# Summing k's features: four tiles added on GpSimd, and attention's period in three equal rounds

## The chip, the cores and the metric

The kernel runs on one core of one Trainium2 chip. A core has a matrix engine (TensorE, PE in the profile, with its weight loads listed apart as PEld), three engines for elementwise work (VectorE or DVE, ScalarE or ACT, GpSimd or POOL) and a queue on SyncE (SP) from which this kernel issues all of its DMA transfers. The engines run side by side, each through its own list of instructions in order, and wait for each other on semaphores. The metric is the device time of one launch in microseconds, lower is better. Before the change it is 1194.68 us, the median of three runs (1191.11 to 1195.12).

## What is computed

Linear attention with a feature map of exponentials over 8 batches of 8 heads, and on its output a two-layer block.

```python
def phi(x):
    proj = np.einsum('bhsd,df->bhsf', x, w_phi)
    proj = proj - np.max(np.abs(proj), axis=-1, keepdims=True)
    return np.concatenate([np.exp(proj), np.exp(-proj)], axis=-1)
q_p, k_p = (phi(q), phi(k))                      # q, k, v: (8, 8, 576, 64); 2 x 128 features
kv  = np.einsum('bhsf,bhsd->bhfd', k_p, v)
z   = np.sum(k_p, axis=2)                        # the feature sums
num = np.einsum('bhsf,bhfd->bhsd', q_p, kv)
den = np.einsum('bhsf,bhf->bhs', q_p, z)[..., None] + 1e-06
x   = num / den                                  # gathered to 4608 x 512
h   = x @ w_in                                   # 512 -> 2048
out = (h - np.tanh(h)) @ w_out                   # 2048 -> 512
```

The change concerns `z`, and the order in which attention's work is issued. The block behind it is computed as before.

## The kernel before

**Units and tiles.** Attention is cut into 32 units of two heads (`e` = 0, 1). q and k of a unit lie transposed in one tile `qk`, 64 rows for each head, with 1152 columns: 576 of q and then 576 of k, which is nine tiles of 128 positions. Tiles 0 to 3 are q; tile 4 is half q's last 64 positions and half k's first 64; tiles 5 to 8 are k.

**What a unit goes through.** `project` multiplies position tiles with `w_phi` into a PSUM tile `pp`, whose one buffer holds a round of up to four tiles of both heads. Behind the products VectorE takes the largest magnitude of each row (`m`, line 207) and subtracts it (`t`, line 209), and only then may the next round overwrite `pp`. There are three rounds, of four, two and three tiles. `q_side` turns q's four and a half tiles on TensorE (`ptr`, `ptt`) and takes their exponentials into `qe` on ScalarE; `k_exp` takes k's into `kp`, which has five tiles (0 is the half one, valid in rows 64 to 127) times two signs of 128 features. `kv` (line 246) multiplies v with `kp` into `pc`. `ksum` (line 254) makes the feature sums as products of a block of ones with each of the five tiles of `kp`, four products of 128 columns for each tile (two heads times two signs), 20 in all, into the third quarter of `pc`. ScalarE copies both out (`kvt`, `kst`), `turn` transposes them on TensorE, and VectorE copies the turned tile into `kv` (line 279). `num` (line 291) and `denom` (line 306) multiply `qe` with that. The denominators travel to another layout and back by DMA: `dd` to `dn`, one reciprocal on VectorE (`den_recip`, lines 334 and 335), `rn` to DRAM (`rr`), and from there spread over the partitions (`rb`). On POOL `den_mul` (line 344) multiplies the numerators `d` with `rb`, and `x_store` writes the result to DRAM.

**The weights.** `w_in` and `w_out` arrive as 64-bit floats. In each period one tile of 128x512 is decoded to float32: one step on ScalarE (`dec_0`), three on VectorE (`dec_1`, lines 166 to 168) and a fourth (`dec_2`, line 172). The first 14 decoded tiles are also split into a high and a low part during attention (`split_w`): ScalarE rounds, POOL subtracts (line 93).

**The order.** Attention runs under a manual schedule, so the lists of all engines are what `period(i)` writes down. Period i does rounds 0 to 2 of unit i, kv and q's side of unit i-1, numerators and denominators of unit i-2, and the division of unit i-3. The feature sums of unit i-1 are the last thing on TensorE in period i; their copy and turn fall into the next period, so `turn` handles the products of unit i-1 and the sums of unit i-2 together, and VectorE's copy of them comes ahead of round 2. On POOL a period has the division and, in the first 14, the subtraction of the weight split. On SP a period has `dn`'s load, the next unit's `qk`, the store of x, `rr`, the two `rb` loads, `v`, and the next raw weight tile.

**Buffers that matter.** `ps_d` has three PSUM banks for everything short-lived (`ptr`, `ptk`, `pd`, `po`). `t2` (the subtracted k tiles of round 2) has one buffer; `d` and `rb` have two.

**Behind attention** the two-layer block runs 192 steps (12 groups of three token tiles, 16 slices of the hidden width), in which the remaining weight tiles are split.

## Time and profile before

One execution was profiled. It took 1192.87 us; its trace spans 1191.1 us from the first to the last instruction, at a mean granted TensorE clock of 0.999.

| stretch | length, us | PE busy | DVE busy | ACT busy | POOL busy |
|---|---|---|---|---|---|
| attention, 100 to 150 us | 50 | 48.90 | 40.81 | 35.85 | 10.78 |
| attention, 250 to 300 us | 50 | 49.32 | 39.92 | 32.07 | 7.07 |
| change of stage, 380 to 400 us | 20 | 16.45 | 17.55 | 12.46 | 14.72 |
| second stage, 600 us to the end | 591 | 585.79 | 419.71 | 404.98 | 143.27 |

The first product of the second stage starts at 371.52 us. The line numbers are those of the kernel before. In the views below a row gives a start and a duration in microseconds, the engine, the line, the operation with output and inputs, and in square brackets how long the engine stood idle ahead of it and who ended that. "x40" behind a product of four-byte floats counts two passes for each of 20 products. PEld rows are weight loads, which run beside products. A product is quoted with the rows and columns of the array that it uses: 64\*128 is half the rows.

### The profile page before, as it was taken

What the parts mean: (1) busy time and instruction counts of PE and PEld (TensorE: products, weight loads), DVE (VectorE), ACT (ScalarE), POOL (GpSimd) and SP (SyncE); (2) the same over time, 40 slices, a digit from 0 to 9 for tenths busy, and PEclk for the clock granted to TensorE, in tenths of its full rate; (3) what the DMA queues carried; (4) which work ended last, traced back from release to release, by engine and by line L of the source; (5) the groups of instructions that cost most, each with busy time, mean ns of one, the idle gap of its engine ahead of it and who ended that gap; (6) DMA issues with size and microseconds to landing.
All of it is one profiled execution on the core that took longest, in us unless ns stands there. A gap on an engine that the chain in (4) does not pass through costs nothing.

```text
span 1191.1 us, 22549 instructions
## 1 busy us (share of the span) xinstructions
PE 1164.2 (98%) x8584; PEld 974.0 (82%) x8584; DVE 883.9 (74%) x1458; ACT 807.4 (68%) x1748; POOL 288.4 (24%) x266
## 2 busy tenths in 40 slices
PE   7999999999998999999999999999999999999998
PEld 5666666666766879999999999999999999999997
DVE  6888887778785988777776777777776777777665
ACT  4667766666766767677766667677766667677665
POOL 0122221011112663222222222222222222222222
PEclk9999999999999999999999999999999999999999
DMA  4465566656552101000100101010100101000000
GB/s 160 146 200 185 178 198 184 182 188 201 170 176 87 33 13 41 14 34 14 35 20 8 40 14 40 14 35 14 36 19 7 40 15 40 14 28 1 28 2 26
DMA packets 51180, 85.70 MB, mean 72 GB/s; under 512 B 13312, under 2 KB 28032, under 8 KB 51072
## 3 DMA queue, kind: packets, MB, share of 16 engines
q1 hardware_dynamic: 51072, 84.27, 22.6%
q8 instruction: 67, 1.10, 0.4%
q14 instruction: 41, 0.34, 0.1%
HBM read 65.08 MB, written 19.02 MB: 71 GB/s over the span
## 4 chain that ended last, share of the span: by engine, by line
PE 87%; DVE 7%; issue 2%; ACT 1%; POOL 1%; DMA 1%; SPq 0%; DVEq 0%; POOLq 0%; ACTq 0%
PE ph L479 32%; PE po L516 11%; PE po L514 11%; PE po L513 11%; PE pp L202 7%; PE pc L246 5%; PE po L291 4%; PE pc L254 3%; PE pd L306 3%; DVE t L209 2%; DVE m L207 2%; PE ptt L215 1%; DVE s L496 1%; DVE dec_ai L167 0%; DVE s L500 0%
## 5 line engine op out<-in xcount | busy, mean ns | idle before, releaser
L507 POOL TENSOR_TENSOR gl<-s,gh 128x384 fp32r<-128x384 f32 x192 | 197.0, 1026 | 568.1 <-ACT gh L506 563.8
L479 PE MATMUL ph<-xh,wli 128*128 128x384 f32 x768 | 259.6, 338 | 1.3 <-POOL wli L93 1.3
L479 PE MATMUL ph<-xh,whi 128*128 128x384 f32 x768 | 259.1, 337 | 0.0
L479 PE MATMUL ph<-xl,whi 128*128 128x384 f32 x768 | 258.1, 336 | 0.0
L486 ACT ACTIVATE y<-ph 128x384 f32<-128x384 f32 x192 | 94.4, 492 | 238.2 <-PE ph L479 238.2
L495 DVE SCALAR_TENSOR_TENSOR s<-s,y 128x384 f32<-128x384 f32 x192 | 107.2, 559 | 166.8 <-ACT s L488 166.7
L513 PE MATMUL po<-who,gh 128*128 128x512 f32 x576 | 227.6, 395 | 1.6 <-ACT gh L506 1.6
L514 PE MATMUL po<-wlo,gh 128*128 128x512 f32 x576 | 227.3, 395 | 0.0
L516 PE MATMUL po<-who,gl 128*128 128x512 f32 x576 | 164.3, 393 | 4.4 <-POOL gl L507 4.4
L500 DVE COPY_PREDICATED s<-mk,th 128x384 f32<-128x384 uint32 x192 | 140.8, 733 | 20.1 <-DVE th L499 0.5
L479 PEld LDWEIGHTS ph<-xh,whi 128*128 128x128 f32 x768 | 144.6, 188 | 8.9 <-issue 0.5
L479 PEld LDWEIGHTS ph<-xl,whi 128*128 128x128 f32 x768 | 144.3, 188 | 8.3
L479 PEld LDWEIGHTS ph<-xh,wli 128*128 128x128 f32 x768 | 144.2, 188 | 2.0 <-POOL wli L93 1.9
L207 DVE TENSOR_REDUCE m<-pp 128x8 f32<-128x1024 f32 (+2 forms) x96 | 91.6, 954 | 65.1 <-PE pp L202 65.1
L516 PEld LDWEIGHTS po<-who,gl 128*128 128x128 f32 x576 | 107.9, 188 | 30.5 <-POOL gl L507 5.7
L496 DVE SCALAR_TENSOR_TENSOR s<-s,s 128x384 f32<-128x384 f32 x192 | 116.0, 604 | 21.2 <-ACT s L490 1.8
L513 PEld LDWEIGHTS po<-who,gh 128*128 128x128 f32 x576 | 108.3, 188 | 20.3 <-ACT gh L506 3.2
L514 PEld LDWEIGHTS po<-wlo,gh 128*128 128x128 f32 x576 | 108.5, 188 | 16.4
L490 ACT ACTIVATE s<-y,bias_t 128x384 f32<-128x384 f32 x192 | 117.9, 614 | 4.7 <-POOL gl L507 4.5
L494 ACT ACTIVATE mk<-y,bias_t 128x384 f32<-128x384 f32 x192 | 117.7, 613 | 2.8 <-DVE s L500 2.8
L488 ACT ACTIVATE s<-y,bias_t 128x384 f32<-128x384 f32 x192 | 118.4, 617 | 0.0
L344 POOL TENSOR_TENSOR rb<-d,rb 128x576 f32<-128x576 f32 x32 | 45.9, 1433 | 292.0 <-DMA rb<-rr 253.7
(66 smaller groups left out, 1640.1 us busy)
## 6 DMA issues: line engine op xcount, KB each, us to landing
qk<-in_qkT SPq DMA_DIRECT2D x31, 576.0 KB, 5.8
v<-in_v SPq DMA_DIRECT2D x32, 320.0 KB, 3.6
rb<-rr SPq DMA_DIRECT2D x64, 144.0 KB, 3.4
xs<-rb SPq DMA_DIRECT2D x32, 288.0 KB, 2.1
x<-xs SPq DMA_DIRECT2D x48, 192.0 KB, 2.3
out<-o SPq DMA_DIRECT2D x36, 256.0 KB, 2.0
rawi<-in_moe_w_in SPq DMA_DIRECT2D x16, 512.0 KB, 4.6
rawo<-in_moe_w_out SPq DMA_DIRECT2D x16, 512.0 KB, 4.4
```

Source lines behind the costliest of these rows:

```text
L207: nc.vector.tensor_reduce(m, x, AX.X, ALU.max, apply_absolute_value=True)
L479: nc.tensor.matmul(h, wt[:, c * P : (c + 1) * P], x[:, c, 0:N], start=(i == 0), stop=(i == 3 * NCT - 1))
L488: nc.scalar.activation(s1, y, AF.Square, bias=bias_t[:, 0:1])
L490: nc.scalar.activation(s2, y, AF.Square, bias=bias_t[:, 1:2])
L494: nc.scalar.activation(mk, y, AF.Relu, bias=bias_t[:, 2:3])
L495: nc.vector.scalar_tensor_tensor(s1, s1, PC1, y, ALU.add, ALU.mult)
L496: nc.vector.scalar_tensor_tensor(s2, s2, PC2, s1, ALU.add, ALU.mult)
L500: nc.vector.copy_predicated(gs, mk.bitcast(U32), th)
L507: pin(nc.gpsimd.tensor_tensor(gl, gs, f32(gh), ALU.subtract))
L513: nc.tensor.matmul(po[t], a, wo[f][0], start=(f == 0), stop=False)
L514: nc.tensor.matmul(po[t], a, wo[f][1], start=False, stop=False)
L516: nc.tensor.matmul(po[t], gl[:, t * P : (t + 1) * P], wo[f][0], start=False, stop=(f == NF - 1))
```

## The change

**The sums.** `kadd` adds four of the five tiles of `kp` (1 to 4) on POOL in three steps of 128x512, into the buffer of the unit's `t2`, which its exponentials have read by then. `ksum` then needs eight products: four over that sum, with all 128 rows, and four over the half tile, with 64. They go into a PSUM bank of their own, `pk`. The last unit keeps the five tiles. Since `t2` has one buffer, the subtraction of the next unit's round 2 now waits for those four products.

**The period.** `project` does three tiles in every round, and the subtraction is a function of its own (`less_max`), so that it can be placed. Round 0 is followed by the numerators, round 1 by kv, round 2 by the sums, q's transposes, the turn and the denominators. Sums and products of one unit are turned together. VectorE's copy of the turned tile is the last thing in its period, behind the decode. The division of a unit comes a period later and stands first in POOL's period, ahead of the adds; the store of x follows the next reciprocals' loads. The subtraction of a weight split stands last in POOL's period: a copy of one column of the freshly decoded tile (`mark`) makes POOL wait for the decode. The third decode step moves from `dec_1` to `dec_2`. In the second period (i = 1) the decode stays behind q's side, which now puts it ahead of the copy of the turned tile.

```diff
@@ split_w
-        pin(nc.gpsimd.tensor_tensor(wl, w, f32(wh), ALU.subtract))
         d[f] = (wh, wl)
+        def low():
+            pin(nc.gpsimd.tensor_tensor(wl, w, f32(wh), ALU.subtract))
+        return low
...
+        def dec_done(u):
+            nc.gpsimd.tensor_copy(mark, u.w[:, 0:1])
...
-        ROUNDS = ((0, 4), (4, 6), (6, 9))
         def project(u, r):
-            j0, j1 = ROUNDS[r]
-            n = j1 - j0
...
-            for a in range(n):
-                j = j0 + a
+            for a in range(3):
+                j = 3 * r + a
...
+        def less_max(u, r):
+            t = p2.tile([P, 2, 3, F], F32, tag=f"t{r}", name=f"t{u.i}_{r}", bufs=1 if r == 2 else 2)
+            nc.vector.tensor_tensor(t, u.x, u.m.unsqueeze(3).broadcast_to([P, 2, 3, F]), ALU.subtract)
...
+        def kadd(u):
+            x = u.t[2].rearrange("p e a f -> p (e a f)")[:, 0 : 4 * F].rearrange("p (e s f) -> p e s f", e=2, s=2)
+            nc.gpsimd.tensor_tensor(x, u.kp[:, :, 2], u.kp[:, :, 3], ALU.add)
+            nc.gpsimd.tensor_tensor(x, x, u.kp[:, :, 4], ALU.add)
+            nc.gpsimd.tensor_tensor(x, x, u.kp[:, :, 1], ALU.add)
+            u.ss = x
         def ksum(u):
-            for j in KT:
-                r = slice(SR, P) if j == 0 else slice(0, P)
+            u.pk = ps_d.tile([P, 512], F32, tag="po", name=f"pk{u.i}")
+            parts = [(slice(0, P), u.ss)] if u.ss is not None else [(slice(0, P), u.kp[:, :, j]) for j in KT[:-1]]
+            parts.append((slice(SR, P), u.kp[:, :, 0]))
+            for a, (r, x) in enumerate(parts):
                 for n in range(4):
...
@@ period, the order as it is now
+            if r: den_recip_load(r)
+            if i + 1 < NU: load(units[i + 1])
+            if q: den_mul(q)
+            if a: project(a, 0); less_max(a, 0)
+            if c: k_exp(c, 2); kadd(c)
+            if p: num(p); num_copy(p)
+            dec_0(dec[i])
+            if a: project(a, 1); less_max(a, 1)
+            if c: kv(c); kv_copy(c)
+            if r: den_recip(r)
+            if q: x_store(q)
+            if i + 1 < NU: load_v(units[i + 1])
+            if a: k_exp(a, 1)
+            dec_1(dec[i])
+            if a: project(a, 2)
+            if c: ksum(c); ksum_copy(c)
+            if a: less_max(a, 2)
+            if c: q_side(c); turn(c)
+            dec_2(dec[i])
+            if low: dec_done(dec[i]); low()
+            if i < NU - 2: dec.append(dec_load(i + 2))
+            if p: denom(p); denom_copy(p)
+            if c: turn_copy(c)
```

In the list of the period conditions and the special first and last periods are shortened; a, c, p, r and q are the units i to i-4.

**TensorE, the stretch between kv and the sums of a period.** Before, in period 23 (`pc` is kv and, on line 254, the sums; `pp` a round; `ptr`, `ptt`, `ptk` transposes; `pd` denominators):

```order
L246 MATMUL pc22_3518<-kp22_3336,v22_3241 64x256 x10
L202 MATMUL pp23_1_3540<-wph_117,qk23_3331 128x128 x4
L221 MATMUL ptr22_3552<-ident_60,t22_1_3399 128x64 x2
L215 MATMUL ptt22_0_3555<-ident_60,t22_0_3348 128x128 x4
L215 MATMUL ptt22_1_3560<-ident_60,t22_0_3348 128x128 x4
L276 MATMUL ptk22_3571<-ident_60,kvt22_3549 128x128 x2
L276 MATMUL ptk22_3571<-ident_60,kst21_3482 128x128
L202 MATMUL pp23_2_3579<-wph_117,qk23_3331 128x128 x6
L306 MATMUL pd21_3594<-qe21_3403,kv22_3575 32x288 x8
L254 MATMUL pc22_3518<-kp22_3336,ones_111 32x128 x20
L202 MATMUL pp24_0_3633<-wph_117,qk24_3479 128x128 x8
```

The same stretch after, in period 19 (`pk` is the sums):

```order
L253 MATMUL pc18_2806<-kp18_2623,v18_2548 64x256 x10
L206 MATMUL pp19_2_2834<-wph_118,qk19_2620 128x128 x6
L271 MATMUL pk18_2843<-t18_2_2714,ones_111 32x128 x4
L271 MATMUL pk18_2843<-kp18_2623,ones_111 32x128 x4
L228 MATMUL ptr18_2857<-ident_60,t18_1_2664 128x64 x2
L222 MATMUL ptt18_0_2860<-ident_60,t18_0_2633 128x128 x3
L222 MATMUL ptt18_0_2860<-ident_60,t18_1_2664 128x128
L222 MATMUL ptt18_1_2865<-ident_60,t18_0_2633 128x128 x3
L222 MATMUL ptt18_1_2865<-ident_60,t18_1_2664 128x128
L287 MATMUL ptk18_2876<-ident_60,kvt18_2817 128x128 x2
L287 MATMUL ptk18_2876<-ident_60,kst18_2852 128x128
L318 MATMUL pd17_2885<-qe17_2716,kv17_2756 32x288 x8
```

Round 2 has moved up behind kv, the sums ahead of q's transposes, from 20 products to eight, and the turn takes products and sums of the same unit.

**POOL, a period with a weight split.** Before, two periods and a half (`rb` is the division, `wli` and `wlo` the low parts of split weights):

```order
L93 TENSOR_TENSOR wli2_837<-wi2_738,whi2_836 128x512
L344 TENSOR_TENSOR rb3_982<-d3_811,rb3_982 128x576
L93 TENSOR_TENSOR wlo2_989<-wo2_890,who2_988 128x512
L344 TENSOR_TENSOR rb4_1134<-d4_963,rb4_1134 128x576
L93 TENSOR_TENSOR wli3_1141<-wi3_1042,whi3_1140 128x512
```

After, from one marker to behind the next (`t5_2` holds the sum of `kp5`):

```order
L184 COPY mark_113<-wo2_874 128x1
L96 TENSOR_TENSOR wli2_784<-wi2_729,whi2_783 128x512
L356 TENSOR_TENSOR rb2_817<-d2_635,rb2_817 128x576
L260 TENSOR_TENSOR t5_2_847<-kp5_753 128x512
L261 TENSOR_TENSOR t5_2_847<-t5_2_847,kp5_753 128x512
L262 TENSOR_TENSOR t5_2_847<-t5_2_847,kp5_753 128x512
L184 COPY mark_113<-wi3_1019 128x1
L96 TENSOR_TENSOR wlo2_929<-wo2_874,who2_928 128x512
```

The three adds have come in behind the division, and the split now waits behind a marker for the newest decoded tile.

**VectorE, one period.** Before, in period 18 (`m` and `t` are a round's reduce and subtract, `dec` and `wi` the decode, `rn` the reciprocals, `kv` the copy of the turned tile):

```order
L207 TENSOR_REDUCE m18_0_2754<-pp18_0_2745 128x8
L209 TENSOR_TENSOR t18_0_2756<-pp18_0_2745,m18_0_2754 128x1024
L166 TENSOR_SCALAR dec_ai9_2760<-dec_ai9_2760 128x512
L167 TENSOR_SCALAR dec_ai9_2760<-dec_ai9_2760 128x512
L168 SCALAR_TENSOR_TENSOR dec_ai9_2760<-rawi9_2556,dec_ai9_2760 128x512
L334 TENSOR_SCALAR rn15_2790<-dn15_2737 128x9
L335 RECIPROCAL rn15_2790<-rn15_2790 128x9
L207 TENSOR_REDUCE m18_1_2805<-pp18_1_2800 128x4
L209 TENSOR_TENSOR t18_1_2807<-pp18_1_2800,m18_1_2805 128x512
L279 COPY kv17_2835<-ptk17_2831 128x384
L207 TENSOR_REDUCE m18_2_2846<-pp18_2_2839 128x6
L209 TENSOR_TENSOR t18_2_2848<-pp18_2_2839,m18_2_2846 128x768
```

After, from round 0's subtraction on:

```order
L216 TENSOR_TENSOR t18_0_2633<-pp18_0_2624,m18_0_2631 128x768
L211 TENSOR_REDUCE m18_1_2662<-pp18_1_2655 128x6
L216 TENSOR_TENSOR t18_1_2664<-pp18_1_2655,m18_1_2662 128x768
L346 TENSOR_SCALAR rn15_2680<-dn15_2618 128x9
L347 RECIPROCAL rn15_2680<-rn15_2680 128x9
L171 TENSOR_SCALAR dec_ai9_2653<-dec_ai9_2653 128x512
L172 TENSOR_SCALAR dec_ai9_2653<-dec_ai9_2653 128x512
L211 TENSOR_REDUCE m18_2_2701<-pp18_2_2694 128x6
L216 TENSOR_TENSOR t18_2_2714<-pp18_2_2694,m18_2_2701 128x768
L175 SCALAR_TENSOR_TENSOR dec_ai9_2653<-rawi9_2463,dec_ai9_2653 128x512
L177 SCALAR_TENSOR_TENSOR wi9_2741<-rawi9_2463,dec_ai9_2653 128x512
L294 COPY kv17_2756<-ptk17_2736 128x384
```

The first two decode steps have moved from behind round 0 to behind round 1 and the reciprocals, the third to behind round 2, and the copy of the turned tile from ahead of round 2 to the period's end.

More of the change, by code (lines that the diff above doesn't have):

```diff
@@ L138, in tile_linear_attention_moe @@
         nc.vector.memset(ones, 1.0)
+        mark = p1.tile([P, 1], F32, name="mark")
         class Dec:
@@ L262, in ksum_copy, with turn, turn_copy @@
         def ksum_copy(u):
+            u.kst = p1.tile([P, F], F32, tag="kst", name=f"kst{u.i}")
+            nc.scalar.copy(u.kst, u.pk[:, 0:F])
+        def turn(u):
+            u.pt = ps_d.tile([P, 512], F32, tag="po", name=f"ptk{u.i}")
+            for a, x in enumerate([u.kvt[:, 0, :], u.kvt[:, 1, :], u.kst]):
+                nc.tensor.transpose(u.pt[:, a * P : (a + 1) * P], x, ident)
+        def turn_copy(u):
             if u.i < NU - 1:
[L264 removed]
+                t = p1.tile([P, 3, P], F32, tag="kv", name=f"kv{u.i}")
             else:
[L266 to L283 removed]
+                t = p2.tile([P, PC], F32, tag="qk", name=f"kv{u.i}")[:, 0 : 3 * P].rearrange("p (a c) -> p a c", a=3)
+            nc.vector.tensor_copy(t.rearrange("p a c -> p (a c)"), u.pt[:, 0 : 3 * P])
+            u.kv, u.ks = t, t[:, 2, :]
         def num(u):
@@ L375, in period @@
         def period(i):
-            a, c, p, p2_ = unit(i), unit(i - 1), unit(i - 2), unit(i - 3)
-            if p2_:
-                den_recip_load(p2_)
+            a, c, p, r, q = (unit(i - n) for n in range(5))
+            if r:
+                den_recip_load(r)
             if i + 1 < NU:
                 load(units[i + 1])
-            if unit(i - 4):
-                x_store(unit(i - 4))
+            if q:
+                den_mul(q)
             if i == NU - 2:
@@ L428, in period @@
                 project(a, 2)
+            if c:
+                ksum(c)
+                ksum_copy(c)
+            if a:
+                less_max(a, 2)
+            if c:
+                q_side(c)
+                turn(c)
             if i < 2:
@@ L553, in tile_linear_attention_moe @@
             while late and late[0] <= 2 * AHEAD + i * NL // (NF - 1):
-                split_w(late.pop(0), pin)
+                split_w(late.pop(0), pin)()
             if i >= 2:
```

88 lines of the change are left out of this document (35 added, 53 removed).

## The prediction

> **What bounds the kernel now.** I read the page's first part, then the chain of work over one steady period of the attention stage, then the timeline of the same period for the weight loads, VectorE (DVE) and GpSimd (POOL).
>
> ```profile
> PE 1164.2 (98%) x8584; PEld 974.0 (82%) x8584; DVE 883.9 (74%) x1458; ACT 807.4 (68%) x1748; POOL 288.4 (24%) x266
> 211.94 0.94 PE pp L202 x12
> 212.87 1.11 PE pd L306 x16
> 213.98 1.23 PE pc L254 x40
> 215.21 1.09 PE pp L202 x16
> 216.30 2.09 PE po L291 x16
> 218.39 2.31 PE pc L246 x20
> 220.69 0.65 PE pp L202 x8
> 221.34 0.11 PE ptr L221 x2
> 221.45 1.02 PE ptt L215 x8
> 222.48 0.34 PE ptk L276 x3
> 222.82 0.13 issue
> 222.95 0.94 PE pp L202 x12
> ```
>
> From one third round (x12) to the next is 222.95 - 211.94 = 11.01 us, and the chain stays on TensorE throughout: in attention a period costs what TensorE's list costs. The list runs 31 times, from unit to unit; the second stage isn't touched by the change. So the question is what the list costs afterwards, and whether another engine then becomes later than it.
>
> ```profile
> 211.90 0.78 PEld L202 LDWEIGHTS pp<-wph,qk 64*128 64x128 f32 x12 [0.36 <-PE ptk L276]
> 213.56 1.03 PEld L254 LDWEIGHTS pc<-kp,ones 128*32 128x32 f32 x32
> 214.78 0.15 PEld L254 LDWEIGHTS pc<-kp,ones 64*32 64x32 f32 x8 [0.20 <-issue]
> 215.13 0.97 PEld L202 LDWEIGHTS pp<-wph,qk 64*128 64x128 f32 x16 [0.20 <-issue]
> 220.62 0.52 PEld L202 LDWEIGHTS pp<-wph,qk 64*128 64x128 f32 x8 [0.39 <-issue]
> 364.63 0.20 PEld L221 LDWEIGHTS ptr<-ident,t 64*128 64x128 f32 x2 [0.20 <-issue]
> ```
>
> The feature sums take their time in weight loads: 32 full-height ones in 1.03 us, 0.032 each. And where products on 64 rows follow others, the load stands idle first: 0.36 behind the turning transposes, 0.39 behind kv's 64-row tail, 0.20 behind the sums' 64-row tail, whether a round or (364.63) the short transposes come next.
>
> **TensorE's list.** Three of four full-height tile groups go: 24 of 32 loads, 24 x 0.032 = **-0.77 us** a period. The rounds keep 18 products in all, so 3+3+3 costs what 4+2+3 did. The order gives some back. The short transposes now follow the sums' tail: **+0.20**. Round 2 now stands behind kv's tail as round 1 did (0.39 stays). Rounds 0 and 1 stand behind full-height denominators and numerators, where no round stands now: between 0 and 0.39 each by the rows above; I take 0.36, the row behind full-height transposes, in place of the 0.36 and 0.20 that go: **+0.16** (bounds -0.56 to +0.22). Together -0.41, between -1.13 and -0.35: a period of **10.6 us**.
>
> [...]
>
> ```profile
> 212.91 0.96 DVE L207 TENSOR_REDUCE m<-pp 128x6 f32<-128x768 f32 x1 [0.53 <-PE pp L202]
> 213.90 0.96 DVE L209 TENSOR_TENSOR t<-pp,m 128x768 f32<-128x768 f32 x1
> 214.78 0.68 DVE L172 SCALAR_TENSOR_TENSOR wi<-rawi,dec_ai 128x512 uint32<-128x512 uint32 x1
> 211.82 0.56 DVE L279 COPY kv<-ptk 128x384 f32<-128x384 f32 x1
> 220.80 0.37 ACT L260 COPY kvt<-pc 128x256 f32<-128x256 f32 x1 [1.96 <-PE pc L246]
> ```
>
> Is DVE in time? Every round is now 0.96 + 0.96. Behind round 0 that is 0.94 + 1.92 + some 0.2 of hand-overs = 3.06 to round 1; TensorE gets there in 0.94 + 2.09 + the gap, about 3.3. Behind round 1 kv (2.31) covers it. Behind round 2 DVE has 1.92 + two decode steps (1.36) + the copy (0.56) + 0.2 = 4.0 before the next numerators; TensorE's list over that stretch (sums about 0.5, transposes 1.13, turn 0.34, denominators 1.11, gap 0.36, round 0 0.94) is 4.4. It fits with 0.2 to 0.4 to spare, **if nothing holds DVE**. ACT has the same instructions and waited 1.96 us at one place of the period; k's exponentials and the copies move with their producers and stay covered. [...]
>
> **POOL's list.** It gets three dependent adds of 128x512 a period, and the sums wait for them. No such add is in the trace; the nearest rows are the weight splits, of the same size:
>
> ```profile
> 95.70 1.41 POOL L344 TENSOR_TENSOR rb<-d,rb 128x576 f32<-128x576 f32 x1 [9.62 <-DMA rb<-rr]
> 97.03 0.42 DVE L166 TENSOR_SCALAR dec_ai<-dec_ai 128x512 f32<-128x512 f32 x1
> 97.07 1.51 POOL L93 TENSOR_TENSOR wli<-wi,whi 128x512 fp32r<-128x512 f32 x1
> 97.48 1.39 DVE L167 TENSOR_SCALAR dec_ai<-dec_ai 128x512 uint32<-128x512 uint32 x1
> 98.90 0.69 DVE L168 SCALAR_TENSOR_TENSOR dec_ai<-rawi,dec_ai 128x512 uint32<-128x512 uint32 x1
> 106.73 1.27 POOL L93 TENSOR_TENSOR wlo<-wo,who 128x512 fp32r<-128x512 f32 x1
> ```
>
> Alone 1.27, beside a DVE decode step 1.51; three adds are 3.8 to 4.5, I take 3.9. The collision costs DVE more: the step at 97.48 lasts 1.39 instead of 0.42, to 0.29 behind POOL's end. Everything on DVE behind it (round 2's reduce and subtract, decode, the kv copy) waits with it, and then TensorE's numerators.
>
> In the 14 periods with a weight split POOL and DVE close a ring: split 1.27, division 1.41, adds 3.9, the held decode step 0.29, reduce and subtract 1.92, two decode steps 1.36, hand-overs about 0.5 = 10.65, and 0.42 more where the other decode step slips between two adds. Between 10.6 and 11.1; I take 10.75: 0.15 over TensorE's list for 13 periods, **+2.0**.
>
> ```profile
> 209.45 0.22 DVE L335 RECIPROCAL rn<-rn 128x9 f32<-128x9 f32 x1
> 209.69 0.33 SPq L336 DMA_DIRECT2D rr<-rn  x1
> 212.40 1.10 SPq L339 DMA_DIRECT2D rb<-rr  x2
> 216.24 1.42 POOL L344 TENSOR_TENSOR rb<-d,rb 128x576 f32<-128x576 f32 x1 [9.08 <-DMA rb<-rr]
> 99.71 0.22 DVE L335 RECIPROCAL rn<-rn 128x9 f32<-128x9 f32 x1
> 105.35 1.41 POOL L344 TENSOR_TENSOR rb<-d,rb 128x576 f32<-128x576 f32 x1 [6.77 <-DMA rb<-rr]
> ```
>
> The division now stands **ahead of the adds** on POOL and waits for its reciprocals: 6.57 us from the reciprocal's end in one period, 5.42 in another. Afterwards a reciprocal ends about 0.8 ahead of its own period's sums (round 1, its 1.92 and 0.39 on DVE against round 1, kv and round 2 on TensorE), so until the next period's sums there are 10.6 + 0.8 = 11.4, less division and adds (1.41 + 3.9 + 0.1): the transfers may take 6.0. In SP's queue the store of x now stands behind the reciprocals' loads instead of between the unit's load and their store, and the reciprocals come later behind that load, so I take 5.4 to 6.0: **0**. Beyond it every us costs half a us a period, as the wait lies in every second step of the ring.
>
> **Once each.**
>
> ```profile
> 21.35 2.06 ACT L226 ACTIVATE qe<-ptt 128x512 f32<-128x512 f32 x4
> 22.01 0.41 DVE L279 COPY kv<-ptk 128x256 f32<-128x256 f32 x1
> 24.31 0.67 ACT L162 ACTIVATE dec_ao<-rawo 128x512 f32<-128x512 f32 x1
> 367.21 1.18 PE L306 MATMUL pd<-qe,kv 128*32 128x288 f32 x16 [0.79 <-DVE kv L279]
> ```
>
> In the second period the kv copy ran before the decode. Now it stands behind four decode steps on DVE (0.42 twice, 0.69, 0.68: 2.2) that start only behind q's exponentials and the decode on ACT: 2.06 + 0.67 + 2.2 + 0.5 = 5.4, against 0.34 + 1.11 + 0.94 and a gap that TensorE has left. That is 2.5 to 3, **+2.5**. In the last period the denominators no longer wait 0.79 for a copy: **-0.8**. Smaller first pieces of k and q save at most some 0.2.
>
> Sum: 31 x -0.41 + 2.0 + 2.5 - 0.8 = **-9.0 us**. The profiled execution took 1192.87 (span 1191.1), so 1183.9; the median of the runs is 1.8 above it, and I say **1185**.
>
> **Rivals.**
> *The division comes late.* Transfers of 6.57 give 10.6 + 0.57/2 = 10.9 a period, 31 x -0.11 + 1.7 = -1.7; at 7 us 11.1 and +4. So 1190 to 1198, about 1192. For it: these rows, and POOL's idle time ends on that transfer now. Against: the store of x is out of the way.
> *POOL's adds hold everything (slower).* If the adds run at the collided 1.51, the ring of the split periods is 10.75 + 0.72 = 11.45, and in the others a transfer of 6.57 and 0.72 more give 10.6 + 1.29/2 = 11.25: 13 x 0.44 + 17 x 0.24 + 1.7 = +11.5, **1205**. It decides from about 1.4 an add. For it: DVE's decode steps lie just where the adds run. Against: 1.27 at 106.73. [...]
> *The gaps at rounds 0 and 1 don't appear.* Then TensorE's list is 9.9 to 10.2, and POOL's rings rule at 10.5 to 10.75: 13 x -0.26 + 17 x -0.5 + 1.7 = -10, down to 1178 with the smaller bounds.
>
> **How the numbers follow.** Forecast 0.46, late division 0.28, slow adds 0.18, no gaps 0.08. 0.5% is 6 us, about what a measurement of this kernel can tell from no change. The forecast lies mostly beyond that, with 0.05 inside; the late division lies mostly inside it. So faster 0.53, same 0.28, slower 0.19. The range goes from the third rival's side, 1177, to 1204, just short of the slow adds' middle.
>
> **What would show it.** The sums' weight loads: 8 full-height ones in about 0.26. The adds at 1.27 to 1.32. Behind denominators and numerators, idle weight loads of 0.3 to 0.4 before a round. Rounds from unit to unit 10.6 apart late in attention and about 10.75 early. If TensorE's sums wait for POOL late in attention, the division or the adds are to blame, told apart by when the division starts; if its numerators wait for the kv copy, DVE was held. I am wrong in the large if a decode step on DVE regularly takes over 1 us.

## The result, and the profile after

After the change the kernel takes 1209.43 us (median of 4 runs, 1207.02 to 1212.56) against 1194.90 before (the three runs given above and a fourth): 1.3% slower, ratio 1.013 (95% interval 1.0096 to 1.0163). The prediction was 1185, with 1177 to 1204 as its range: wrong in size and in sign. The profiled execution took 1207.02, its span 1205.0, 13.9 above the span before.

The first part of the page of after (busy time, share of the span, instructions):

```profile
PE 1165.4 (97%) x7840; PEld 957.3 (79%) x7840; DVE 891.9 (74%) x1458; ACT 804.6 (67%) x1748; POOL 407.8 (34%) x373
```

PE issues 744 fewer products than before and is busy 1.2 us longer. POOL has the adds: 119 us more. Where the 13.9 us lie is read from ScalarE's copies of kv's products (`kvt<-pc`), one a unit, and from the first product of the second stage (`ph`):

| | before | after | difference so far |
|---|---|---|---|
| copy of unit 0 | 18.9 | 24.2 | +5.3 |
| copy of unit 1 | 31.0 | 40.1 | +9.1 |
| copy of unit 2 | 42.7 | 50.8 | +8.1 |
| copy of unit 31 | 364.93 | 377.28 | +12.4 |
| first `ph` | 371.52 | 384.39 | +12.9 |
| end of the span | 1191.1 | 1205.0 | +13.9 |

So there are two main losses: about 8 us in the first three periods, and 4.3 over the 29 periods from unit 2 to unit 31, where 29 x 0.41 = 12 had been expected as a gain. The last 1.5 us come behind unit 31. A period is (377.28 - 50.8) / 29 = 11.26 us. Two of the 29 took 13.54 and 13.84, with a stretch of low granted clock in each (0.50 from 98.5 to 101.5 us and from 245.5 to 248.5); the other 27 average 11.08.

The weight loads of two periods of after (start, duration, line, operation; in brackets the idle time ahead):

```profile
257.17 0.16 PEld L271 LDWEIGHTS pk<-t,ones 128*32 128x32 f32 x8
257.53 0.15 PEld L271 LDWEIGHTS pk<-kp,ones 64*32 64x32 f32 x8 [0.20 <-issue]
257.88 0.20 PEld L228 LDWEIGHTS ptr<-ident,t 64*128 64x128 f32 x2 [0.20 <-issue]
...
260.61 0.75 PEld L206 LDWEIGHTS pp<-wph,qk 64*128 64x128 f32 x12 [0.47 <-DVE dec_ao L175]
...
263.72 0.75 PEld L206 LDWEIGHTS pp<-wph,qk 64*128 64x128 f32 x12 [0.44 <-PE po L303]
...
267.04 0.75 PEld L206 LDWEIGHTS pp<-wph,qk 64*128 64x128 f32 x12 [0.38 <-issue]
```

The list is as forecast: eight full-height loads (0.16 us, where 0.26 was expected), and an idle gap ahead of each round and of the short transposes. From 257.17 to the same row a period on (267.91) it is 10.74 us; the next period, from the copy at 267.22 to the one at 277.93, is 10.71. TensorE can go at 10.7; it mostly doesn't. The groups of after's TensorE from 60 to 370 us, 28 periods (busy, mean ns | idle time before them and who ended it):

```profile
L303 PE MATMUL po<-qe,kv 128*64 128x288 f32 x432 | 58.3, 411 | 7.7 <-DVE kv L294 7.5
L271 PE MATMUL pk<-t,ones 128*32 128x128 f32 x224 | 12.0, 285 | 6.2 <-POOL t L262 6.0
```

The sums wait 6.2 / 28 = 0.22 a period for POOL's third add, the numerators 7.7 / 28 = 0.27 for DVE's copy. 10.71 + 0.49 = 11.2, nearly the 11.26 measured. What makes the adds late shows in the timeline of one of the later periods of after, behind the last weight split (POOL, DVE and the queue SPq):

```profile
205.55 1.29 POOL L260 TENSOR_TENSOR t<-kp 128x512 f32<-128x512 f32 x1
206.92 1.28 POOL L261 TENSOR_TENSOR t<-t,kp 128x512 f32<-128x512 f32 x1
208.28 1.27 POOL L262 TENSOR_TENSOR t<-t,kp 128x512 f32<-128x512 f32 x1
208.32 1.25 DVE L346 TENSOR_SCALAR rn<-dn 128x9 f32<-128x9 f32 x1
209.61 0.22 DVE L347 RECIPROCAL rn<-rn 128x9 f32<-128x9 f32 x1
209.86 0.33 SPq L348 DMA_DIRECT2D rr<-rn  x1
211.72 1.11 SPq L351 DMA_DIRECT2D rb<-rr  x2
215.58 1.41 POOL L356 TENSOR_TENSOR rb<-d,rb 128x576 f32<-128x576 f32 x1 [6.03 <-DVE m L211]
216.94 1.30 POOL L260 TENSOR_TENSOR t<-kp 128x512 f32<-128x512 f32 x1
218.32 1.27 POOL L261 TENSOR_TENSOR t<-t,kp 128x512 f32<-128x512 f32 x1
219.57 0.17 DVE L346 TENSOR_SCALAR rn<-dn 128x9 f32<-128x9 f32 x1
219.67 1.27 POOL L262 TENSOR_TENSOR t<-t,kp 128x512 f32<-128x512 f32 x1
```

At 208.32 DVE begins to add 1e-6 to the reciprocals' nine columns. It starts 0.04 behind POOL's third add and ends 0.02 behind it: 1.25 us instead of 0.17. Only then come the reciprocal, the transfers (209.83 to 215.58, 5.75), the division and the next unit's adds, whose third ends at 220.94. From end to end that is 220.94 - 209.55 = 11.39 us: **a ring once a period**, through POOL, DVE and the DMA, longer than TensorE's 10.7. (The page names `m` as what ended POOL's wait; that had long been done, the last to come was `rb`.) At 219.57 the next small add slips in between two adds and takes 0.17. Over attention (27 of them; ns, shortest, median, longest):

```profile
L346 DVE TENSOR_SCALAR rn<-dn x27: 163/770/1255, 50.1 to 343.8; 128x9 f32<-128x9 f32 x27
L347 DVE RECIPROCAL rn<-rn x27: 215/216/218, 50.5 to 344.8; 128x9 f32<-128x9 f32 x27
```

Before, the small add's row reads 161/168/173. The reciprocal of the same nine columns takes the same time in all 27 units, but here it mostly runs behind the third add and not beside it; experiment 1 shows it beside one.

In the periods with a weight split the ring is another. There the split stands ahead of the division on POOL, and the 12 divisions from 57 to 183 us don't wait for the transfers: POOL stands at most 1.25 us ahead of one, and under 0.2 ahead of eight of them. It waits at the marker instead:

```profile
118.83 1.27 POOL L262 TENSOR_TENSOR t<-t,kp 128x512 f32<-128x512 f32 x1
119.15 0.98 DVE L346 TENSOR_SCALAR rn<-dn 128x9 f32<-128x9 f32 x1
...
124.47 0.18 POOL L184 COPY mark<-wo 128x1 f32<-128x1 f32 x1 [4.37 <-DVE wo L177]
...
125.84 1.41 POOL L356 TENSOR_TENSOR rb<-d,rb 128x576 f32<-128x576 f32 x1
```

The small add is held to the end of the third add (120.13 against 120.10). Behind it on DVE come the reciprocal, two decode steps, round 2's reduce and subtract and the last two decode steps, 4.37 us in all; then the marker, the split, the division and the next adds, whose third ends at 129.95 + 1.27 = 131.22. That ring is 131.22 - 120.10 = 11.12 us, on POOL and DVE alone. Both rings pass through the held small add.

The start, in after's timeline of TensorE and DVE, with rows of late attention for comparison:

```profile
19.09 0.94 PE L206 MATMUL pp<-wph,qk 64*128 64x128 f32 x12 [2.24 <-DVE t L216]
19.96 4.19 PE L253 MATMUL pc<-kp,v 128*64 128x256 f32 x20
...
29.25 0.43 DVE L171 TENSOR_SCALAR dec_ao<-dec_ao 128x512 f32<-128x512 f32 x1 [2.14 <-ACT dec_ao L167]
...
31.51 0.55 DVE L294 COPY kv<-ptk 128x384 f32<-128x384 f32 x1
32.21 4.11 PE L303 MATMUL po<-qe,kv 128*64 128x288 f32 x16 [4.00 <-DVE kv L294]
...
261.63 2.16 PE L303 MATMUL po<-qe,kv 128*64 128x288 f32 x16
...
264.59 2.53 PE L253 MATMUL pc<-kp,v 128*64 128x256 f32 x20
```

kv stands behind round 1 now, and round 1 waits 2.24 us for DVE (before, kv ran in that wait). The numerators wait 4.00 us for the copy behind the decode. And in and behind both waits the granted clock falls (0.66 and 0.52 in the windows shown with experiment 13): the products take 4.19 for 2.53 and 4.11 for 2.16, 3.6 us more for these two groups alone.

### The profile page after: what moved, and what is told of

The parts are those of the page before. It is cut to its first block, busy times and chain, and to the rows that moved or that the text cites. A ratio compares the mean times of both kernels' runs of the same rounds, so it can differ in the third digit from the quotient of the medians.

```text
span 1205.0 us, 21125 instructions
## 1 busy us (share of the span) xinstructions
PE 1165.4 (97%) x7840; PEld 957.3 (79%) x7840; DVE 891.9 (74%) x1458; ACT 804.6 (67%) x1748; POOL 407.8 (34%) x373
## 4 chain that ended last, share of the span: by engine, by line
PE 72%; DMA 7%; DVE 7%; POOL 2%; ACT 2%; issue 1%; SPq 1%; DVEq 0%; POOLq 0%; ACTq 0%
PE ph L501 32%; PE po L538 10%; PE po L536 10%; PE po L535 10%; DMA dn<-dd 5%; PE po L303 2%; PE pc L253 2%; PE pp L206 2%; DMA rr<-rn 1%; PE ptt L222 1%; ACT qe L233 1%; PE pk L271 1%; DVE t L216 1%; DVE rn L346 1%; DVE m L211 1%
## 5 line engine op out<-in xcount | busy, mean ns | idle before, releaser
L522 DVE COPY_PREDICATED s<-mk,th 128x384 f32<-128x384 uint32 x192 | 142.2, 740 | 20.5 <-ACT y L508 0.5
L211 DVE TENSOR_REDUCE m<-pp 128x6 f32<-128x768 f32 x96 | 91.6, 954 | 56.2 <-PE pp L206 56.0
L206 PEld LDWEIGHTS pp<-wph,qk 64*128 64x128 f32 x1152 | 73.1, 189 | 47.8 <-issue 25.6
```

The lines of the kernel that those rows point to most:

```text
L211: nc.vector.tensor_reduce(m, x, AX.X, ALU.max, apply_absolute_value=True)
L522: nc.vector.copy_predicated(gs, mk.bitcast(U32), th)
```

## The experiments

In the expectations **A** is the first ring shown: POOL's adds hold DVE's small add, and the division stands ahead of the adds. **B** blames the division's place alone: the adds are late because they stand behind a division that waits for its transfers. **C** (also D) is the start's two waits. Unless said otherwise an edit is made on the kernel after the change; every ratio is to the kernel before in the same batch (medians 1193.0 to 1194.0, 1194.90 for after), with its 95% interval. Periods are from copy to copy of kv's products, the early ones from unit 2 to unit 13, the late ones from unit 14 to unit 30. The copies and periods of a row come from one profiled execution, in which a stretch of half clock (last section) can lengthen single periods by 2 to 3 us (13.54 and 13.84 in after, where the others average 11.08).

| kernel | median, us | ratio | copy of unit 2, us | mean period, early / late, us |
|---|---|---|---|---|
| before | 1194.90 | 1 | 42.7 | 11.17 / 11.03 |
| after | 1209.43 | 1.013 (1.0096-1.0163) | 50.8 | 11.31 / 11.20 |
| 1 constant on ScalarE | 1196.64 | 1.0024 (1.001-1.0039) | 50.2 | 10.84 / 10.96 |
| 2 division behind adds | 1202.20 | 1.0079 (1.0052-1.0105) | 48.5 | 11.16 / 11.14 |
| 3 five tiles, no adds | 1207.35 | 1.0122 (1.0098-1.0147) | 49.2 | 11.36 / 11.37 |
| 4 copy ahead of decode | 1206.28 | 1.0114 (1.0092-1.0137) | 50.4 | 11.56 / 11.13 |
| 5 start edit | 1201.88 | 1.0077 (1.0054-1.01) | 45.6 | 11.52 / 11.14 |
| 6 start edit + constant | 1190.54 | 0.9981 (0.9966-0.9996) | 44.5 | 11.08 / 10.94 |
| 7 before + adds | 1239.03 | 1.0377 (1.0356-1.0398) | 44.4 | 13.20 / 12.18 |
| 8 before + adds + constant | 1224.56 | 1.0267 (1.0242-1.0291) | 43.5 | 12.23 / 11.82 |
| 9 sums behind q's turns | 1204.98 | 1.011 (1.0078-1.0143) | 48.4 | 10.99 / 11.37 |
| 10 = 6 + sums behind q's turns | 1189.51 | 0.9969 (0.9953-0.9984) | 48.3 | 10.78 / 10.86 |
| 11 = 10 + last decode step later | 1194.43 | 1.0007 (0.9993-1.002) | 44.6 | 10.90 / 11.08 |
| 12 before + constant | 1192.72 | 0.9993 (0.9981-1.0006) | 43.4 | 11.07 / 11.03 |
| 13 = 6 + idle products | 1188.68 | 0.9961 (0.995-0.9973) | 43.0 | 10.96 / 10.79 |
| 14 = 13 + sums behind q's turns | 1187.03 | 0.994 (0.9916-0.9965) | 43.8 | 10.91 / 10.87 |

**1. The constant added by ScalarE.** DVE's small add goes; the denominators get their 1e-6 in the copy that ScalarE makes anyway.

```diff
-            nc.scalar.copy(u.dd, u.pd[:, 0:CH])
+            nc.scalar.activation(u.dd, u.pd[:, 0:CH], AF.Identity, bias=bias_t[:, 3:4])
...
-            pin(nc.vector.tensor_scalar_add(rn, dn, 1e-6))
-            nc.vector.reciprocal(rn, rn)
+            pin(nc.vector.reciprocal(rn, dn))
```

> The kernel after the change, with the 1e-6 added by ScalarE in the copy of the denominators, so that VectorE has only the reciprocal itself and no small add ahead of it (in the kernel after, that add of 128x9 has a mean of 646 ns, 201 before, and ends with POOL's third add). Theory A, a ring through that add: POOL's third add ends, the small add is let go, transfers of 5.3 to 5.8 us, division 1.41, three adds 3.9, which is about 11.1 us a period. Then the period goes from 11.1 to 10.7 or 10.8, the second stage starts some 10 us earlier than at 384.4, and the time falls by about 10 us. Theory B, the division is late by its place in POOL's list alone: the period stays at 11.0 to 11.1 and the time falls by at most 3 us.

The first `ph` comes at 374.74 instead of 384.39, 9.65 us earlier, with the start as late as in after. Its reciprocal takes what it takes alone:

```profile
L347 DVE RECIPROCAL rn<-dn x27: 203/206/217, 60.3 to 344.3; 128x9 f32<-128x9 f32 x27
```

One instruction of 0.17 us a unit costs about 10 us of the whole (10.6 by the spans, 1.06% by the ratios). Part of it is the slow clock: behind unit 2 no period here is over 12.0, so after's two of 13.54 and 13.84 have no like. B gives no such gain. In this kernel the reciprocal runs wholly beside an add in 26 of the 27 units, and it is the decode step behind it that is held now, 1.39 for 0.37:

```profile
114.69 1.27 POOL L263 TENSOR_TENSOR t<-t,kp 128x512 f32<-128x512 f32 x1
114.73 0.20 DVE L347 RECIPROCAL rn<-dn 128x9 f32<-128x9 f32 x1
114.85 1.39 DVE L172 TENSOR_SCALAR dec_ao<-dec_ao 128x512 f32<-128x512 f32 x1
```

The marker then waits 4.09 instead of 4.37, and the period is 10.84 instead of 11.12. The late periods, 10.96 in the mean, are still 0.25 above TensorE's 10.71: from 182 to 370 us its sums wait 3.9 us for the third add and its numerators 2.4 for the copy.

**12. The same edit before the change.**

```diff
-            nc.scalar.copy(u.dd, u.pd[:, 0:CH])
+            nc.scalar.activation(u.dd, u.pd[:, 0:CH], AF.Identity, bias=bias_t[:, 3:4])
...
-            pin(nc.vector.tensor_scalar_add(rn, dn, 1e-6))
```

> The kernel before the change with ScalarE adding the denominator's constant, nothing else. There POOL has no adds and DVE's small add takes 0.20 us; the edit takes that 0.2 us from DVE, which is not the bound: within 1.5 us of the kernel before (by theory A the constant costs something only beside the adds). If it gains more than 3 us, the 9.7 us that the same edit gave after the change were not the adds' doing.

Periods of mostly 11.02 as before, ratio 0.9993 with 1 inside its interval. The small add costs something only beside the adds.

**2. The division behind the adds** (`d` with three buffers, one decoded-weight buffer fewer for the room).

```diff
-            if q:
-                den_mul(q)
             if i == NU - 2:
...
                 if i < NU:
                     kadd(c)
+            if q:
+                den_mul(q)
```

> The kernel after the change, with the division behind the three adds on POOL instead of ahead of them (d has three buffers for it, and the pool of weight tiles one tile less to make room). Theory B (the division's place): the adds start as soon as k's exponentials end, TensorE's sums never wait for POOL, and the period goes to 10.7; the second stage starts near 372. Theory A (VectorE is held by the adds): the ring is open too, but the small add and the decode steps are still held behind the adds, so VectorE stays late with round 2 and the copy; the period stays at 11.0 to 11.2.

The sums' wait is gone and the period isn't shorter than 11.1. TensorE's groups from 182 to 370 us (17 periods), and the small add:

```profile
L303 PE MATMUL po<-qe,kv 128*64 128x288 f32 x272 | 36.7, 411 | 8.1 <-DVE kv L294 8.1
...
L271 PE MATMUL pk<-t,ones 128*32 128x128 f32 x136 | 7.2, 285 | 0.0
```

```profile
L346 DVE TENSOR_SCALAR rn<-dn x27: 172/878/1345, 58.6 to 350.0; 128x9 f32<-128x9 f32 x27
```

The hold stays (median 0.88), and what it delays on DVE ends in the copy for the numerators: 8.1 / 17 = 0.48 a period. So with the division out of the way the hold is paid for at another place. As the whole cause B falls. The edit does gain 0.5%, though: unit 2 comes 2.3 us earlier, and no period is over 12.4, where after has two above 13.5. How much of that is the division's place and how much the clock isn't settled.

**9. The sums behind q's turns.** TensorE does the ten turns of q between round 2 and the sums, and the denominators ahead of kv's turn: 1.4 us more before it needs POOL.

```diff
-            if c:
-                ksum(c)
-                ksum_copy(c)
             if a:
                 less_max(a, 2)
             if c:
                 q_side(c)
-                turn(c)
+                ksum(c)
+                ksum_copy(c)
...
             if c and i < NU:
+                turn(c)
                 turn_copy(c)
```

> After, with the feature sums moved behind the query side's ten turns and the denominators moved ahead of the turn of kv: TensorE has 1.4 us more work between the projection's last round and the sums, so that it need not stand for POOL's third add (0.96 to 1.56 us in the periods where the clock fell to half). Nothing of POOL's own ring (third add, DVE's small add, two transfers, division, adds) is changed. Theory A: the ring still closes at about 11.1 and only the few periods of 13 us go, 1-2 of them in a run: 1203-1207, periods 11.1-11.25. Rival T (TensorE's wait for the third add, and the half clock behind it, is the cost, not the ring): periods 10.7-10.8, about 1193-1197.

Neither number came: 10.99 early, 11.37 late. The small add tells why, in the stretches 60 to 182 and 182 to 370 us:

```profile
L346 DVE TENSOR_SCALAR rn<-dn x11: 161/162/986, 70.5 to 179.6; 128x9 f32<-128x9 f32 x11
...
L346 DVE TENSOR_SCALAR rn<-dn x16: 173/690/1103, 190.4 to 361.4; 128x9 f32<-128x9 f32 x16
```

Early, with the split's subtraction ahead of the adds on POOL, the small add falls between two adds, takes 0.16, and eight periods are 10.83 to 10.85, the split ring without the hold as in experiment 1. Without the subtraction it is held again, and the periods are long (one of the late ones is 14.46; the others average 11.16). So A's ring isn't a constant of the order, as I had written: it closes where the small add meets an add. And TensorE's own wait for the third add isn't the main cost: from 60 to 370 us it fell from 6.0 to 0.5 us, while the numerators' wait for DVE's copy rose from 7.5 to 11.4.

**3. The new order with five tiles and no adds.**

```diff
                 k_exp(c, 2)
-                if i < NU:
-                    kadd(c)
```

> The kernel after the change without the adds on POOL: the sums take five tiles on TensorE as before, in the new order. Theory C, the new order alone costs the time: the period is no shorter than 11.1 although nothing holds VectorE, and is 10.7 + 0.77 = 11.4 to 11.5 by TensorE's list, 0.4 above that of the kernel before, the second stage starts near 390. Theory A: the same TensorE list, but the small add back at 0.2 us and no wait of the sums for POOL; that is, the order costs 0.4 a period and the adds give back no more than that.

Every period is 11.36 or 11.37, the small add 0.17. Two copies of kv's products in its timeline:

```profile
265.05 0.37 ACT L277 COPY kvt<-pc 128x256 f32<-128x256 f32 x1 [1.66 <-PE pc L253]
276.41 0.37 ACT L277 COPY kvt<-pc 128x256 f32<-128x256 f32 x1 [2.54 <-PE pc L253]
```

So the order by itself lengthens TensorE's list by 11.36 - 11.02 = 0.34, and the adds take 11.36 - 10.71 = 0.65 from it.

**7. Before's order with the adds alone** (their sum in a tile of its own, one decoded-weight buffer fewer), and **8.** with ScalarE's constant as well.

```diff
             if c:
                 k_exp(c, 2)
+                if i < NU:
+                    kadd(c)
             if 2 <= i < NU:
                 dec_0(dec[i])
                 dec_1(dec[i])
```

> Before's order and its rounds of four, two and three tiles; only the three adds on POOL and the shorter sums are taken over (the sum in a tile of its own, one decoded-weight buffer fewer to make room). It parts the change into its order and its adds. If the new order's own list (11.36 with five-tile sums against 11.02) is what the adds' saving of 0.65 has to pay for, the old order gets periods below 11.0: 10.4 to 10.7 if nothing else closes, 1175-1185. By theory A (a one-period ring over POOL, the held small add of DVE and the transfers) the old order pays as well: there the reciprocal and the division stand in the same period, and the adds held against DVE's small steps give 11.0 to 11.2 again: 1190-1197. Start near before's 42.7 in both.

> As the kernel before this one, with ScalarE adding the denominator's constant. By theory A the small add's stall goes from 0.5-0.8 us to nothing and the periods shorten by 0.1-0.4: 1182-1192. If POOL's adds hold only the decode steps in this order, it equals the kernel without the edit within 1.5 us.

Both far outside: 46 and 31 us slower than before. Here three decode steps of DVE stand right where the adds run. The tile view of the second one in 7 (before: median 426 ns):

```profile
L167 DVE TENSOR_SCALAR dec_ao<-dec_ao x12: 1372/1376/1381, 68.6 to 348.4; 128x512 uint32<-128x512 uint32 x12
```

It is held every time, the third step (0.69 before) for 1.64 in most periods as well, and TensorE's rounds wait 43.2 us for DVE's subtractions between 60 and 370 us, of the 46 that are lost. DVE, which fills the decoded-weight buffers, waits for none of them. So the new order isn't a by-product: it carries most of the decode away from the adds, and what was left beside them was the small add (and, in seven of 28 periods, the first decode step, at 1.30 to 1.44). In 7 the small add is held in seven of 28 units; why its going saves 15 us in 8 wasn't traced.

**4. The start: the copy ahead of the decode** in the second period.

```diff
+            if c and i < 2:
+                turn_copy(c)
             if i < 2:
                 dec_0(dec[i])
                 dec_1(dec[i])
...
-            if c and i < NU:
+            if c and 2 <= i < NU:
                 turn_copy(c)
```

> The kernel after the change, with the copy of the turned tile ahead of the decode in the second period, as it was before the change. Theory D, the start: TensorE's wait of 4.0 us ahead of the first numerators goes, and with it the halved clock behind it (the first numerators took 4.11 us instead of 2.16); the second stage starts 4 to 7 us earlier, with the later periods as they were. Without theory D (the wait only moves to the next round): at most 1 us.

Nothing gained: unit 2 at 50.4. The four decode steps now stand ahead of the next period's round 0 on DVE, and TensorE stands 3.22 us there instead of 4.00. The wait moved.

**5. The start, both places:** in the second period kv ahead of round 1, and the decode where the later periods have it.

```diff
-            if 2 <= i < NU:
+            if 1 <= i < NU:
                 dec_0(dec[i])
...
+            if c and i == 1:
+                kv(c)
+                kv_copy(c)
             if a:
                 project(a, 1)
                 less_max(a, 1)
-            if c:
+            if c and i > 1:
                 kv(c)
                 kv_copy(c)
...
-            if 2 <= i < NU:
+            if 1 <= i < NU:
                 dec_1(dec[i])
...
-            if i < 2:
+            if i < 1:
                 dec_0(dec[i])
                 dec_1(dec[i])
```

> After, with two edits in the second period alone: the first unit's second product (kv) and its copy stand ahead of the projection's second round, as before the change, and the decode steps of that period stand where the later periods have them, so that only the last one is left ahead of the copy that the numerator waits for. Theory C (the start's 8 us come from these two places, 2.24 and 4.00 us of standing TensorE, and from the products at half the clock behind each): the first kv copy moves from 24.2 to 19-20, the third from 50.8 to 45 or earlier, the slices from 20 to 40 us show a granted clock near 1.0, and the whole is 4 to 8 us earlier than after, about 1202-1205. Rival S (the new order's pipeline is longer to fill, or the loads set the start): the waits move on, the third copy stays at 49-51, under 2 us gained. Neither touches the periods from 3 on: 11.2-11.3 again.

Unit 2 comes 5.2 us earlier, the first `ph` 3.3: the periods behind it give 1.9 back, one of them with 13.74. The first copy (20.5) and the third (45.6) are a little later than expected, and the clock still falls, to 0.66 from 25 to 30 us. C holds for most of the start.

**6. Start edit and constant together.**

```diff
+            nc.scalar.activation(u.dd, u.pd[:, 0:CH], AF.Identity, bias=bias_t[:, 3:4])
...
+            if c and i == 1:
+                kv(c)
+                kv_copy(c)
...
-            if i < 2:
+            if i < 1:
                 dec_0(dec[i])
```

> The same start edit, and the denominator's small constant added by ScalarE in its copy, so that DVE's small add, which POOL's adds hold, is gone. If the ring and the start are two separate costs of the change, they add: 1196.6 of the kernel with ScalarE's constant alone less 4 to 8 = 1189-1193, that is 2 to 5 below before; by rival S 1195-1197. Periods 10.85 / 10.96 as with the constant alone.

By the ratios, against after, the constant is worth 1.06%, the start edit 0.53%, both in one kernel 1.49%: two separate costs that add up. The kernel is level with before or slightly faster.

**10. The same with the sums behind q's turns,** their copy between ScalarE's two pairs of q's exponentials (and the turn behind the denominators, as in 9).

```diff
-            for e in range(2):
-                q_exp(c, e, pts[1 + e])
+            q_exp(c, 0, pts[1])
+            ksum(c)
+            ksum_copy(c)
+            q_exp(c, 1, pts[2])
```

> The start edit, ScalarE's constant, and the sums behind the query side's turns with their copy between ScalarE's two pairs of query exponentials. With the ring open (10.85-10.95 with ScalarE's constant) what is left above TensorE's list of 10.70 is its waits for the third add and the slow clock behind the longest (13.35 in one period of the start-and-constant kernel: 0.96 us standing, then 1.7 at half clock). If so the periods are 10.7-10.8 throughout, no period over 11.5, and the time 1182-1187. If the moved turn of kv makes the numerator wait instead (its copy on DVE stands behind two decode steps), periods 10.9-11.0 and no gain, 1189-1192.

Nearly every period is 10.77 or 10.78, as expected, one late is 11.89; the time is 1189.5 and not 1182 to 1187. In the profiled execution, one of the longer ones at 1192.9, the start was 3.8 us later than in 6 (48.3 against 44.5), though up to kv of the second period the order is the same; the other runs have no profile. In this execution kv's first products took 3.93 us, in 6 they took 2.53, behind the same standing of 2.09: by that length the clock fell in the one and not in the other.

**11. The last decode step behind the numerators' copy,** and with it the split's subtraction and the next raw weight load.

```diff
         def dec_2(u):
             nc.vector.scalar_tensor_tensor(u.a, u.lo, 29, u.a, ALU.logical_shift_right, ALU.bitwise_or)
+
+        def dec_3(u):
             w = wpool.tile([P, DM], F32, tag="w", name=f"w{u.nm}")
...
                 turn_copy(c)
+            if i < NU:
+                dec_3(dec[i])
+            if low:
+                dec_done(dec[i])
+                low()
```

> As the kernel before this one, and the decode's last DVE step behind the copy that the numerator waits for (with it the split's low half and the next raw load, in the 14 split periods). If the numerator waits for that copy in the kernel before, the later periods lose 0.2-0.5 against it: 10.4-10.6, and the split periods, where the low half's subtraction comes 0.7 later on POOL and holds up the division, 10.8-11.1: 1177-1185. If it doesn't wait, equal within 2 us or later by the split periods' 0.2.

A miss: mostly 10.90, 0.12 longer than in 10. The step in front was part of what the numerators waited for, but the wait moved: from 60 to 370 us their wait for the copy falls from 3.6 us in 10 to 0.9, while the rounds, which now find that step ahead of their reduce and subtract on DVE, wait 9.3 us instead of 0.3.

**13. Products of no use in the start's idle places.**

```diff
-            if i == 0:
-                warm(8)
+            if i < 2:
+                warm(8 if i == 0 else 12)
             if a:
                 project(a, 2)
+            if i == 0:
+                warm(12)
```

> The start-and-constant kernel with twelve products of no use (1.6 us at full clock) in each of the two places of the first two periods where TensorE stands for 2.1 us. If the standing makes the clock fall: granted clock 1.00 in all slices from 16 to 34 us, the third kv copy at 42.5-44 instead of 44.5, and 1-2 us off the time: 1188.5-1190. If the clock falls anyway, slices at 0.5 there again and no gain or up to 1 us lost.

Windows of after, of 6 and of 13 (busy time of the five engines, then the granted clock):

```profile
20.00:25.00 5.00, 5.00 (x37) 2.67 (x40) 1.92 (x2) 0.81 (x3) 0.89 (x1) 0.66 0.37 145
25.00:30.00 5.00, 3.21 (x43) 2.38 (x41) 2.63 (x4) 4.68 (x12) 0.00 (x0) 1.00 0.23 66
30.00:35.00 5.00, 2.79 (x12) 1.65 (x14) 3.81 (x6) 0.68 (x1) 3.26 (x4) 0.52 0.47 158
```

```profile
20.00:25.00 5.00, 2.86 (x38) 1.88 (x37) 4.11 (x6) 1.69 (x5) 1.08 (x1) 0.88 0.54 215
25.00:30.00 5.00, 5.00 (x39) 3.63 (x37) 4.14 (x6) 3.92 (x9) 1.98 (x3) 0.78 0.44 148
```

```profile
20.00:25.00 5.00, 4.27 (x52) 3.20 (x50) 4.47 (x7) 2.59 (x7) 0.32 (x1) 1.00 0.36 145
25.00:30.00 5.00, 4.17 (x44) 2.96 (x46) 3.56 (x6) 4.29 (x9) 3.44 (x4) 1.00 0.56 209
```

With the standing filled the clock stays at 1.00 from 10 to 40 us, unit 2 comes at 43.0 (44.5 in 6, 42.7 before), and the whole is 1.9 us shorter in the median, though the intervals of the two ratios overlap. So in this execution the half clock went with the standing. Standing alone doesn't always bring it: before stood 2.09 us at 13 us as well, and its clock was 1.00 from 8 to 20 us.

**14. Everything:** 13, and from the fourth period on the sums behind q's turns.

```diff
+            if c.i > 1:
+                ksum(c)
+                ksum_copy(c)
...
-            if c:
+            if c and i <= 2:
                 ksum(c)
                 ksum_copy(c)
...
+            if c and (i <= 2 or i == NU):
                 turn(c)
```

> The same, and from the fourth period on the sums behind the query side's turns (as in the kernel that gave constant periods of 10.78). If the start and the waits for the third add are separate costs, they add: third copy at 43-45, then 10.78 nearly throughout: 3-4 us below the kernel with constant periods, 1185-1187. If the constant periods came from that kernel's late start (48.3), its phase against the loads for instance, the periods are 10.9-11.0 here and nothing is gained: 1189-1190.

1187.03 us, ratio 0.994 (0.9916 to 0.9965): the fastest of all, 6 us below before and 22 below after. (6, 10 and 13 lie below before with their whole intervals too, by 0.2 to 0.4%.) The periods aren't the constant 10.78 of 10; a few are 11.0 to 11.4, and ahead of its numerators TensorE stands 8.1 us between 60 and 370 us, 6.1 of it for DVE's copy. The two remedies add up only in part.

## Why the prediction was wrong, point by point

**TensorE's list: right.** Predicted 10.6; measured 10.71. The order was to give back 0.36 and gave back 0.34; the shorter sums were to take 0.77 and took 0.65. The gaps at rounds 0 and 1 came, at 0.47 and 0.44 to 0.52 where I took 0.36, so the third rival fell.

**The adds: right.** 1.27 to 1.30 each in the rows above; of all 93 one took over 1.4. They were not slowed, so the second rival's time (1205) was near by luck, for a reason that didn't happen: the adds don't pay, DVE does.

**The transfers: right in the middle, not at the edge.** Behind the last split, where POOL stands for them, 17 of them took 5.26 to 7.14 us from the reciprocal's end to the division, median 5.69, against the 5.4 to 6.0 taken. Ten of the 17 stayed within 6.0, and the division came late all the same. Seven were longer, which is the late division's condition; its part in the late periods isn't told apart from the hold's.

**The split ring: at its upper bound.** Taken at 10.75 between 10.6 and 11.1, it is 11.12 in the period shown and 10.84 without the small add. Behind the third add it counted one held decode step, the reduce and subtract and two more steps, 3.57 us; there were 4.37, as the reciprocal and both first decode steps stand behind the held small add. The marker, for which the sum had no term, costs 0.18.

**The step that failed** begins with this sentence: "Afterwards a reciprocal ends about 0.8 ahead of its own period's sums". It lets the reciprocal run free of POOL. I had quoted a decode step held by a split to 0.29 behind its end, and priced that hold for the decode alone. The small add ahead of the reciprocal is the same operation in the trace (TENSOR_SCALAR), stands in the same stretch, and in 17 of 27 units took over 0.5 us. Held, it ends with the third add. In the periods without a split the two-period ring with 11.4 us of room then becomes a ring of one period and 11.4 us of length; in those with one it adds to the split ring as just said. Experiment 1 shows the size, both rings and the slow clock behind the longest waits together: 9.65 us. "Every us costs half a us a period" fell with it. The sign I had set for being wrong in the large, a decode step regularly over 1 us, did not show it: the first decode step was held in seven of 28 periods, the second in none. The trace gives the hold its size (1.25 us for nine columns beside an add of 1.27, and 0.17 where the step slipped in between two adds) and not its cause. By that size every step of DVE in the stretch had to be gone through, however small, and I had priced the long ones.

**The start: mis-sized**, +2.5 predicted, +8.1 measured. The decode ahead of the copy was seen. Not seen were kv behind round 1, which adds 2.24 us of standing to the first unit, and the half clock behind both waits. With the order put back and the standing filled, unit 2 comes at 43.0 (experiment 13), so the two together account for all but 0.3 of it in that execution.

**The end:** -0.8 predicted, +0.5 measured from the last copy to the first `ph`. That, and the 1.0 us in the second stage, were not looked into.

**DVE's room** of 0.2 to 0.4 before the numerators was not measured by itself. Without the hold and with the longer list of experiment 3 the numerators don't wait for the copy; with the hold they wait 0.27 a period in after.

Left open: the loads of `dn` come late in the new order (DVE stands 14.0 us for them in after's trace); an earlier issue wasn't tried. What the numerators still wait for in experiment 14 isn't settled.

## What to carry to other kernels

When work is given to an engine, look in the trace for instructions of another one that were held beside such work (here a decode step of 0.42 us, at 1.39 beside a split), and list every instruction of the other that can fall beside it, not only the long ones: the nine-column step, in a chain of waits, cost about 10 us of the whole, while with the 512-column decode step held in its stead (1.39 for 0.37, experiment 1) the periods were 10.84 and 10.96, within 0.25 of TensorE's 10.71. Then follow each chain that leaves the held step until it comes back to the engine that holds it; if it comes back within one period, the period can't be shorter than its length. And work out the first two or three periods of a pipeline on their own: a wait there costs its length and can cost a stretch of slow clock behind it (here 2.24 and 4.00 us of standing, and 3.6 us more in the two groups of products behind).

## What was not expected of the hardware

**The clock fell behind short waits.** In steady attention of after TensorE stood 1.18 us, and soon behind that the granted clock fell to 0.61 and 0.53 in two windows of 2 us; in windows of half a us it is 0.50 in each from 98.5 to 101.5:

```profile
97.50 0.43 PE L271 MATMUL pk<-t,ones 128*32 128x128 f32 x8 [1.18 <-POOL t L262]
...
98.48 1.97 PE L222 MATMUL ptt<-ident,t 128*128 128x128 f32 x8
```

```profile
96.00:98.00 2.00, 0.82 (x19) 0.43 (x20) 0.99 (x3) 0.98 (x2) 1.37 (x2) 1.00 0.37 145
98.00:100.00 2.00, 2.00 (x17) 1.73 (x12) 1.83 (x4) 0.99 (x4) 0.00 (x0) 0.61 0.08 11
100.00:102.00 2.00, 2.00 (x18) 1.15 (x20) 1.72 (x3) 1.70 (x4) 0.18 (x2) 0.53 0.54 169
102.00:104.00 2.00, 2.00 (x30) 1.22 (x24) 1.05 (x2) 1.33 (x3) 1.90 (x3) 1.00 0.86 242
```

That period took 13.54 us. The eight transposes, 1.97 here, take 1.09 at 25.92 us, where the clock is 1.00. Behind the same 2.09 us of standing kv's first products took 3.93 us in experiment 10 and 2.53 in 6. Before stood 1.33 us at 66.75 and its clock stayed at 1.00, so the length of a wait alone doesn't decide it. What does, no run here shows.

**A small step was held nearly as long as a large one,** up to 1.25 us for nine columns, against 1.30 to 1.44 for the first decode step's 512 in after, while the reciprocal of the same columns took 203 to 217 ns in experiment 1, where in 26 of 27 units it ran wholly beside an add.
